# Long convolution with gate: the last 4 of the 100 rows of each a_u store issued by GpSimd instead of SyncE

## The chip, the cores and the metric

The kernel runs on one core of a Trainium2 chip. The core has a matrix engine (TensorE, PE in the profile), a vector engine (VectorE, DVE), an activation engine (ScalarE, ACT), a general engine (GpSimd, POOL) and an engine that only issues transfers and waits (SyncE, SP). Sixteen DMA engines carry the transfers between the chip's large memory (DRAM) and the core's own memory (SBUF). Each compute engine and SyncE works through its own list of instructions in order, and an instruction that has to wait holds up everything behind it on that engine.

The metric is the device time of one execution in microseconds (us); lower is better. The time before is the median of three runs.

## The reference

What is computed, cut to the part that matters:

```python
B, S, D = x.shape                                   # 4, 12800, 128
h_filt = (np.maximum(pos_emb @ w1, 0.0) @ w2) * np.exp(-0.01 * np.arange(S))[:, None]
u = x * v
Uf = np.fft.rfft(u, n=2 * S, axis=1)
Hf = np.fft.rfft(h_filt, n=2 * S, axis=0)
y = np.fft.irfft(Uf * Hf[None], n=2 * S, axis=1)[:, :S]
x = x * y                                           # first half of the work
gate = sigmoid(causal_conv5(x, conv_w))             # second half
out = (gate * (x @ w_val)) @ w_out
```

A long causal convolution along the sequence (12800 positions, 128 channels, 4 batches) is followed by a short gated projection. All arithmetic is in 32-bit floats.

## The kernel before

The long convolution is a Fourier transform that is factored over 100 x 64 positions (`N1 = 100`, `N2 = 64`), and the kernel has three stages, each with its own pools of tiles. The stage boundary goes through DRAM: the first stage writes `a_u`, the second reads `a_u` and writes `c_y`, the third reads `c_y` and writes the result.

**First stage.** It has 64 steps, one for each pair (`q`, `s`) with `q` from 0 to 31 and `s` 0 or 1. A step does the following.

- `fetch(n + 7)` issues a transfer of 1024 KB of `xv` (the inputs x and v) from SyncE into one of five buffers (`held`, shown as the tile `ld`).
- `product(n + 3)` multiplies x and v on DVE (line 312).
- `mirrored(q + 1)`, in every other step, forms sums and differences on DVE (line 321, tile `eo`) and a subtraction for each of the two on POOL (line 322).
- `spectra(q, s)` runs matmuls against a constant table (line 334, into `fp`), and ACT copies the result into the tile `st` (line 336). `st` has four buffers (`bufs=4`): the copy of step n needs the store of step n - 4 landed.
- Some work of the filter's own transform is slipped in (`filt()`), so many units to a step: `gp`, `ap` and `ag` are its tiles, and `fk` its tables.
- `store` writes the 100 rows of `st` of the step before to `a_u[:, s, q]`. A row is 2 x 2 x 4 x 128 floats, or 8 KB.

The 100 rows are not stored in one transfer. The helper `_Split` (lines 109 to 118) cuts them into rows 0 to 95 and rows 96 to 99, two transfers of 768 KB and 32 KB, both on SyncE; the profile therefore shows both at the helper's line 118. The same helper, as `sync_s`, serves the loads of `c_y` in the third stage.

**What sets the order.** The stage is inside `tc.manual_schedule()`: each engine gets its instructions in the order in which the code is written. Waits are put in by the framework. A transfer reports its landing on one of eight counters that are handed out in turn (DMAHW0 to DMAHW7 in the listings of the order; the transfers that GpSimd issues have eight of their own, DMASW0 to DMASW7), and a transfer waits until the one that had its counter before has landed. So at most eight transfers of SyncE are under way at a time in this stage. With three transfers a step (fetch, store of 96 rows, store of 4 rows) that is two steps and two thirds.

**End of the stage.** The first loads of `a_u` for the second stage (`load_pair(0, 24)` and `load_a`, line 213) stand in SyncE's list among the last stores; each waits for the stores of the rows that it reads.

Of the kernel before, what the change touches and what calls it, by code (L numbers as in the profile page):

```python
# [24 lines left out]
J, N1, N2 = 2, 100, 64  # L25
# [96 lines left out]
def tile_longconv_gate(  # L122
# [20 lines left out]
    nc = tc.nc  # L143
    sync_s = _Split(nc.sync)
# [4 lines left out]
    a_u = dram.tile([N1, 2, N2 // 2, 2, J, B, D], F32, name="a_u")  # L149
# [82 lines left out]
    with tc.tile_pool(name="p1", bufs=1) as p1, tc.tile_pool(name="ps1", bufs=1, space=PSUM) as ps1:  # L232
# [92 lines left out]
        def spectra(q, s):  # L325
            eo = eos[q]
            st = p1.tile([128, 2, J, B, D], F32, name="st", bufs=4)
            for o in range(2):
                fp = ps1.tile([128, 2, J, XE], F32, name="fp", bufs=2)
                terms = ((0, 0), (2, 1)) if s == o else ((1, 0),)  # L330
                for i, (w, l) in enumerate(terms):
                    for h in range(2):
                        r = slice(h * NH, (h + 1) * NH)
                        nc.tensor.matmul(  # L334
                            out=fp[:, h], lhsT=fold[r, w], rhs=eo[r, o, :, l], start=i == 0, stop=i == len(terms) - 1)
                nc.scalar.copy(out=st[:, o].rearrange("k j (h b) d -> k h j (b d)", h=2), in_=fp)  # L336
            return st

        def store(q, s, st):
            sync_s.dma_start(  # L340
                out=a_u[:, s, q].rearrange("k e j b d -> k (e j b d)"),
                in_=st[:N1].rearrange("k e j b d -> k (e j b d)"))

        fetched, us, eos, last = {}, {}, {}, None
        with tc.manual_schedule():
# [15 lines left out]
            for n in range(N2):  # L361
                q, s = divmod(n, 2)
                if n + XB + 2 < N2:
                    fetch(n + XB + 2)
                if n + 3 < N2:
                    product(n + 3)
                if s == 0 and q + 1 < N2 // 2:
                    mirrored(q + 1)
                st = spectra(q, s)
                while spent < n_fil * (n + 1) / (N2 - 6):  # L370
                    step = next(fil, None)
                    if step is None:
                        break
                    spent += step
                if n == N2 - 2:
                    loaded[0] = load_pair(0, NL)
                if last:
                    store(*last)
                last = q, s, st
                if n == 40:  # L380
                    _narrow(nc, p1, wval, raw_val)
                if n == 46:
                    _narrow(nc, p1, wout, raw_out)
                if n == 52:
                    _narrow(nc, p1, cw, raw_cw)
            for _ in fil:
                pass
            store(*last)


    with tc.tile_pool(name="p2", bufs=1) as p2, tc.tile_pool(name="ps2", bufs=1, space=PSUM) as ps2:
# [67 lines left out]
        with tc.manual_schedule():  # L459
            for p in range(-1, NP + 1):  # L460
# [8 lines left out]
                if p == 41:  # L469
                    j, g = y_order[0]  # L470
                    nc.sync.dma_start(
                        out=xr_first, in_=xt[j][:, g * R:(g + 1) * R].rearrange("d n b a -> d (n b a)"))
# [57 lines left out]
    with tc.tile_pool(name="p3", bufs=1) as p3, tc.tile_pool(name="ps3", bufs=1, space=PSUM) as ps3:  # L530
# [144 lines left out]
        with tc.manual_schedule():  # L675
# [4 lines left out]
            for _ in range(WARM):  # L680
                w_ps = ps3.tile([D, 2 * D], F32, name="o_ps", bufs=2)
                nc.tensor.matmul(
                    out=w_ps, lhsT=ident, rhs=dft.rearrange("p a k -> p (a k)"), start=True, stop=True)
            for t in range(-AHEAD3, NT + 2):
                s = t + AHEAD3
                if s + 1 < NT:
                    load_rows(s + 1)
                if 0 <= s < NT:
                    j, g = y_order[s]
# [80 lines left out]
```

## Time and profile before

| | |
|---|---|
| time, median of 3 runs | 1163.94 us (1157.94 to 1168.69) |
| the profiled execution, its own time | 1167.67 us |
| its span, first to last instruction | 1165.5 us |
| TensorE clock granted, mean | 0.969 |
| PE, DVE, POOL, ACT busy | 90%, 83%, 67%, 53% of the span |
| bytes moved | 344.60 MB, 296 GB/s over the span |

The span lies within the profiled execution's own time; 2.2 us of that time lie outside the span. A row of the profile that groups instructions gives the line of the kernel, the engine, the operation, the tiles (output, an arrow, inputs), their shapes, a count, then the busy time and the mean duration, and after the bar the idle time of the engine just before them with what ended it. SPq is SyncE issuing transfers. In the table by stretches, each row is a stretch of time with the busy time of each engine, the granted clock, the mean busy share of the 16 DMA engines, and the rate at which they moved bytes; a share can come out above 1 where packets overlap. A packet of a DMA engine is the unit in which the profile counts transfers. In the chain of waits a piece "DMA a_u<-st" runs from the issue of a transfer to its landing.

### The profile page before, as it was taken

The page shows a single profiled execution, that of the slowest core. Times are in us where ns is not written, and L with a number is a line of the kernel's source. Part 1 is how long each engine was busy: PE and PEld are TensorE (multiplying, and loading weights), DVE is VectorE, ACT ScalarE, POOL GpSimd, SP SyncE. Part 2 cuts the span into 40 slices and gives each one's busy share as a digit, 9 for nine tenths or more (in the row PEclk, how much of TensorE's full clock was granted, in tenths as well). Part 3 has the DMA queues.
Part 4 walks back from the last instruction along what each step waited for, and adds up shares of the span by engine and source line. Part 5 has one row for each costly group of instructions (what it writes and reads, how often), then busy time and mean ns, then how long its engine had stood idle before and what let it go on. Part 6 is the DMA issues. An engine that isn't in the chain of part 4 may idle for free.

```text
span 1165.5 us, 17562 instructions
## 1 busy us (share of the span) xinstructions
PE 1046.1 (90%) x6208; PEld 492.1 (42%) x6208; DVE 969.3 (83%) x1150; ACT 615.7 (53%) x1000; POOL 775.2 (67%) x393
## 2 busy tenths in 40 slices
PE   4899887887764999999999999979999999999986
PEld 2455543443321444444444444434444444444432
DVE  5675445798944899999999999629999999999996
ACT  1366555665641344444444444346676767677763
POOL 3354332323313888889888889737889898898880
PEclk9999999998995899999999999988999999999999
DMA  9999999999987588988888998558999999999932
GB/s 364 350 417 403 361 352 345 353 341 350 344 268 286 209 311 300 317 300 302 303 312 287 362 339 321 178 176 218 283 288 285 264 292 278 278 289 284 284 119 113
DMA packets 92888, 344.60 MB, mean 296 GB/s; under 512 B 9774, under 2 KB 19418, under 8 KB 77610
## 3 DMA queue, kind: packets, MB, share of 16 engines
q1 hardware_dynamic: 58824, 263.74, 69.1%
q10 hardware_dynamic: 33978, 79.74, 17.8%
q8 instruction: 51, 0.84, 0.3%
q14 instruction: 35, 0.29, 0.1%
HBM read 212.37 MB, written 131.07 MB: 295 GB/s over the span
## 4 chain that ended last, share of the span: by engine, by line
PE 58%; DMA 28%; ACT 6%; DVE 4%; issue 2%; SPq 1%; ACTq 0%; DVEq 0%
PE c_ps L435 21%; DMA a_u<-st 19%; PE sd L596 9%; PE z_ps L419 9%; DMA ld<-in_xv_dram 6%; PE o_ps L657 6%; PE v_ps L647 5%; PE tp L610 5%; PE c_ps L404 2%; DVE gt L638 2%; PE fp L334 2%; ACT gt L635 1%; ACT o_sb L665 1%; DMA c_y<-c_sb 1%; ACT sg L642 1%
## 5 line engine op out<-in xcount | busy, mean ns | idle before, releaser
L623 POOL TENSOR_TENSOR ext<-yr,xr 128x400 f32<-128x400 f32 x120 | 301.6, 2515 | 44.0 <-DVE yr L621 41.9
L322 POOL TENSOR_TENSOR eo<-eo 128x512 f32<-128x512 f32 x62 | 116.8, 1904 | 212.0 <-DVE eo L321 212.0
L334 PE MATMUL fp<-eo,fold 64*128 64x512 f32 x768 | 194.4, 640 | 54.5 <-ACT st L336 40.1
L638 DVE SCALAR_TENSOR_TENSOR gt<-ext,cw,gt 128x1600 f32<-128x1600 f32 x128 | 241.5, 1887 | 0.8 <-ACT gt L635 0.8
L442 ACT COPY c_sb<-c_ps 128x1024 f32<-128x1024 f32 x100 | 101.3, 1013 | 204.6 <-PE c_ps L435 196.5
L336 ACT COPY st<-fp 128x1024 f32<-128x1024 f32 x128 | 124.2, 1015 | 133.2 <-DMA a_u<-st 81.5
L435 PE MATMUL c_ps<-va,ld 64*128 64x512 f32 (+1 forms) x800 | 166.6, 556 | 0.1
L425 DVE TENSOR_TENSOR va<-z_ps,h_sb 128x2048 f32<-128x2048 f32 x50 | 114.3, 2286 | 38.7 <-DMA ld<-a_u 30.4
L504 POOL TENSOR_TENSOR va<-va,vb 128x1024 f32<-128x1024 f32 x50 | 118.4, 2367 | 40.0 <-DVE vb L425 40.0
L419 PE MATMUL z_ps<-ld 64*64 64x512 f32 x800 | 122.4, 621 | 18.2 <-DMA ld<-a_u 16.3
L334 PEld LDWEIGHTS fp<-eo,fold 64*128 64x128 f32 x768 | 74.8, 197 | 135.8 <-issue 76.4
L596 PE MATMUL sd<-ag,inv 100*64 100x512 f32 x512 | 128.7, 620 | 1.6 <-ACT sd_sb L603 1.0
L657 PE MATMUL o_ps<-gd,wout 128*128 128x400 f32 x256 | 112.4, 521 | 19.7 <-DVE gd L652 10.9
L435 PEld LDWEIGHTS c_ps<-va,ld 64*128 64x128 f32 x800 | 74.2, 189 | 113.7 <-issue 110.2
L506 POOL TENSOR_TENSOR va<-va,vb 128x1024 f32<-128x1024 f32 x50 | 118.3, 2367 | 0.0
L603 ACT COPY sd_sb<-sd 128x512 f32<-128x512 f32 x128 | 76.1, 595 | 76.8 <-PE sd L596 54.1
L425 DVE TENSOR_TENSOR vb<-z_ps,h_sb 128x2048 f32<-128x2048 f32 x50 | 114.0, 2280 | 0.0
L647 PE MATMUL v_ps<-ext,wval 128*128 128x400 f32 x256 | 107.1, 500 | 0.0
L435 PE MATMUL c_ps<-vc,ld 64*128 64x512 f32 x400 | 94.2, 589 | 0.0
L610 PEld LDWEIGHTS tp<-ident,sd_sb 128*128 128x128 f32 x512 | 60.1, 144 | 78.9 <-PE sd L596 47.9
L505 POOL TENSOR_TENSOR vc<-vc,vd 128x768 f32<-128x768 f32 x50 | 91.2, 1824 | 2.2 <-issue 0.3
L610 PE MATMUL tp<-ident,sd_sb 128*128 128x128 f32 x512 | 81.9, 286 | 5.4 <-ACT sd_sb L603 3.8
(84 smaller groups left out, 1452.1 us busy)
## 6 DMA issues: line engine op xcount, KB each, us to landing
ld<-in_xv_dram SPq DMA_DIRECT2D x64, 1024.0 KB
c_y<-c_sb ACTq DMA_DIRECT2D x100, 512.0 KB
ld<-a_u SPq DMA_DIRECT2D x49, 1024.0 KB
a_u<-st SPq DMA_DIRECT2D x64, 768.0 KB
ag<-c_y SPq DMA_DIRECT2D x116, 384.0 KB
out_dram<-o_sb ACTq DMA_DIRECT2D x32, 800.0 KB
xr<-in_xt_dram SPq DMA_DIRECT2D x31, 800.0 KB
ld<-in_tab_w_dram SPq DMA_DIRECT2D x12, 768.0 KB
```

What stands on the lines that cost most here:

```text
L334: nc.tensor.matmul(out=fp[:, h], lhsT=fold[r, w], rhs=eo[r, o, :, l], start=i == 0, stop=i == len(terms) - 1)
L336: nc.scalar.copy(out=st[:, o].rearrange("k j (h b) d -> k h j (b d)", h=2), in_=fp)
L419: nc.tensor.matmul(out=zs[c][half[h]], lhsT=wk[half[c], 0, half[h]], rhs=a2[half[c], h, j], start=True, stop=True)
L425: nc.vector.tensor_tensor(out, z.rearrange("p (b d) -> p b d", d=D).unsqueeze(1).to_broadcast([128, n, B, D]), h_sb.unsqueeze(2).to_broadc ...
L435: nc.tensor.matmul(out=c_ps[:, h, 0:n], lhsT=wk[half[h], 1 + c], rhs=vt[half[h]].rearrange("p b d -> p (b d)"), start=(i == 0), stop=(i == ...
L504: nc.gpsimd.tensor_tensor(va[:, 0:2], va[:, 0:2], vb[:, 0:2], op=ALU.add)
L596: nc.tensor.matmul(out=sd[c * N2:(c + 1) * N2], lhsT=inv[:, c], rhs=ct[c][:, r * B * D:(r + 1) * B * D], start=True, stop=True)
L610: nc.tensor.transpose(out=tp[:, b], in_=t[:, b], identity=ident)
L623: nc.gpsimd.tensor_tensor(e[:, r0 + r], yr, xr, op=ALU.mult)
L638: nc.vector.scalar_tensor_tensor(gt, rows(t, k), cw[:, k:k + 1], gt, op0=ALU.mult, op1=ALU.add)
L647: nc.tensor.matmul(out=v_ps, lhsT=wval, rhs=rows(t)[:, r * ROW:(r + 1) * ROW], start=True, stop=True)
L657: nc.tensor.matmul(out=o_ps, lhsT=wout, rhs=gd, start=True, stop=True)
```

## The change

In `store`, the helper is no longer used. Rows 0 to 95 are issued by SyncE as before; rows 96 to 99 are issued by GpSimd. Bytes, rows and destination are the same. The loads of `c_y`, which use the helper too, are untouched.

```diff
         def store(q, s, st):
-            sync_s.dma_start(
-                out=a_u[:, s, q].rearrange("k e j b d -> k (e j b d)"),
-                in_=st[:N1].rearrange("k e j b d -> k (e j b d)"))
+            for eng, r in ((nc.sync, slice(0, 96)), (nc.gpsimd, slice(96, N1))):
+                eng.dma_start(
+                    out=a_u[r, s, q].rearrange("k e j b d -> k (e j b d)"),
+                    in_=st[r].rearrange("k e j b d -> k (e j b d)"))
```

SyncE's list in the middle of the first stage, before the change: a number behind `st` names the copy of a step, a number behind `ld` a buffer of the fetches, and the brackets name what a transfer waits for (a counter's previous transfer, or an engine).

```order
L118 DMA a_u_60<-st_1026 96x2048 [waits DMAHW2_49,Activation_49]
L118 DMA a_u_60<-st_1026 4x2048 [waits DMAHW3_49]
L306 DMA ld_106<-in_xv_dram 128x2048 [waits DMAHW4_49,DVE_49]
L118 DMA a_u_60<-st_1063 96x2048 [waits DMAHW5_49,Activation_49]
L118 DMA a_u_60<-st_1063 4x2048 [waits DMAHW6_49]
L306 DMA ld_102<-in_xv_dram 128x2048 [waits DMAHW7_49,DVE_49]
```

The same place in SyncE's list after the change:

```order
L341 DMA a_u_60<-st_1026 96x2048 [waits DMAHW1_49,Activation_49]
L306 DMA ld_106<-in_xv_dram 128x2048 [waits DMAHW2_49,DVE_49]
L341 DMA a_u_60<-st_1063 96x2048 [waits DMAHW3_49,Activation_49]
L306 DMA ld_102<-in_xv_dram 128x2048 [waits DMAHW4_49,DVE_49]
L341 DMA a_u_60<-st_1097 96x2048 [waits DMAHW5_49,Activation_49]
```

The transfers of 4 rows are gone from it; a step takes two of the eight counters instead of three, so a counter comes round after four steps.

POOL's list at the same place, after the change (before it, the subtractions of `eo` stand there alone, two for every two steps):

```order
L322 TENSOR_TENSOR eo0_110<-eo0_110 128x2x256 [waits DVE_49] x2
L341 DMA a_u_60<-st_1026 4x2048 [waits DMASW1_49,Activation_49]
L341 DMA a_u_60<-st_1063 4x2048 [waits DMASW2_49,Activation_49]
L322 TENSOR_TENSOR eo1_111<-eo1_111 128x2x256 [waits DVE_49] x2
L341 DMA a_u_60<-st_1097 4x2048 [waits DMASW3_49,Activation_49]
L341 DMA a_u_60<-st_1134 4x2048 [waits DMASW4_49,Activation_49]
```

Two transfers of 4 rows now stand between each two pairs of subtractions; each waits for ACT's copy of its `st` and for the GpSimd transfer of eight steps earlier.

## The prediction

> **What bounds the kernel now.** I read the page's chain of waits first, then the table by stretches, then the waits of the stretch that the change touches, and last the packets there. The chain that ended last, by engine and by line:
>
> ```profile
> PE 58%; DMA 28%; ACT 6%; DVE 4%; issue 2%; SPq 1%; ACTq 0%; DVEq 0%
> PE c_ps L435 21%; DMA a_u<-st 19%; PE sd L596 9%; PE z_ps L419 9%; DMA ld<-in_xv_dram 6%; PE o_ps L657 6%; PE v_ps L647 5%; PE tp L610 5%; PE c_ps L404 2%; DVE gt L638 2%; PE fp L334 2%; ACT gt L635 1%; ACT o_sb L665 1%; DMA c_y<-c_sb 1%; ACT sg L642 1%
> ```
>
> The transfers of the first stage hold 25% of the chain (19% stores of a_u, 6% fetches); the later stages are PE's. So transfers set the first stage, some 360 us of the span, and only there does the change act. The table by stretches shows that it has two regimes:
>
> ```profile
> 60.00:120.00 60.00, 56.59 (x562) 33.56 (x562) 38.15 (x30) 38.97 (x45) 29.82 (x14) 1.00 1.01 409
> 120.00:240.00 120.00, 99.54 (x740) 53.79 (x737) 70.97 (x98) 69.98 (x112) 34.70 (x21) 0.96 0.98 351
> 240.00:320.00 80.00, 64.17 (x292) 32.99 (x290) 71.21 (x112) 51.30 (x100) 27.18 (x16) 0.94 0.98 345
> 120.00:320.00 200.00, 163.71 (x1030) 86.78 (x1026) 142.18 (x209) 121.28 (x211) 61.88 (x37) 0.95 0.98 349
> ```
>
> After the length come PE, PEld, DVE, ACT and POOL busy, the clock, the DMA share and GB/s. Up to 120 us the core moves 409 GB/s, then 349, although the mix of transfers is the same and DMA engines look busy all the time (0.98). PE falls from 94% busy to 82%. What the engines wait for between 120 and 320 us:
>
> ```profile
> POOL eo L322 <- DVE eo L321: 138.1, 19, 13.0
> ACT st L336 <- DMA a_u<-st: 60.2, 27, 4.2
> DVE ld L312 <- DMA ld<-in_xv_dram: 16.1, 5, 3.3
> DVE u L312 <- DMA ld<-in_xv_dram: 11.3, 5, 2.6
> ...
> SPq L118 <- DMA ld<-in_xv_dram: 90.8, 38, 3.5
> SPq L306 <- DMA a_u<-st: 59.8, 37, 2.1
> ```
>
> ACT waits 60.2 us for a store to free st, DVE 27.4 us for fetches, and SP 150.6 us of 200 for one of its eight counters. All of that is late landing. The chain shows how late, and what an uncrowded transfer takes:
>
> ```profile
> 148.71 16.37 DMA a_u<-st
> ...
> 165.58 15.20 DMA a_u<-st
> ...
> 340.59 1.35 SPq L213
> ...
> 343.66 11.24 DMA a_u<-st
> ...
> 355.33 4.25 DMA a_u<-st
> ```
>
> In the crowded stretch a store takes 15 to 16 us from issue to landing; the last one, issued when nothing else was left, takes 4.25 us. L213 at 340.59 is the first load of a_u, at the end of the stage.
>
> **Where the 4 rows lie.** The transfers between 133 and 300 us:
>
> ```profile
> DMA packets 8243, 58.38 MB, mean 350 GB/s; under 512 B 1124, under 2 KB 1124, under 8 KB 1124
> ...
> ld<-in_xv_dram SPq DMA_DIRECT2D x32, 1024.0 KB
> a_u<-st SPq DMA_DIRECT2D x31, 768.0 KB
> a_u<-st SPq DMA_DIRECT2D x31, 32.0 KB
> ```
>
> The 1124 packets under 512 B are the reports of landing: the 63 large transfers, at one from each of 16 engines, make 1008, and the 116 left over 31 small transfers are 3.7 each. Beside the reports no packet is under 8 KB, so a row is one packet. The 4 rows are carried by about four engines, not sixteen. A step then loads an engine with (1024 + 768) / 16 = 112 KB, and the four with 120 KB; spread evenly it would be 1824 / 16 = 114 KB. If they are the same four each time, they set the pace while the others run ahead up to eight transfers and then starve, which is what a fall from 409 to 349 GB/s after a while looks like. No row here shows which four they are.
>
> The Trainium skill ("DMA: Bandwidth & Descriptors", section "Why a DMA increments its semaphore by 16 and not by 1") says that a transfer issued by SyncE takes the lowest-numbered engines, as many as divide its rows, and one issued by GpSimd consecutive engines from a cursor that moves on. By that rule the four would be the same before the change and rotate after it; the count of reports above agrees with the number of engines, and nothing in this trace shows the rotation.
>
> **The change part by part.**
>
> *Removed from SP:* 64 issues and their waits for a counter. One issue costs 0.25 to 0.3 us by this row (60 to 320 us, shortest, median, longest, in ns; the longest hold a wait):
>
> ```profile
> L118 SPq DMA_DIRECT2D a_u<-st x101: 245/303/1950, 60.8 to 319.5; - x101
> ```
>
> That is 64 x 0.25 = 16 us of SP's time, taken at 0: SP waits for landings three quarters of the stretch, and that wait stays if the landings are as late. Two of eight counters a step instead of three lets SP run four steps ahead, not 2.7. I take 0 for that too, since the four buffers of st limit the stores to four steps (the 60.2 us wait of ACT); its bounds are 0 and the gain below.
>
> *Added to POOL:* 64 issues. No row shows a transfer issued by GpSimd. From below it is SP's 0.25 us; from above, POOL's idle time: 138.1 us before eo in 120 to 320 us, at 37 steps (349 GB/s x 200 us / 1.868 MB a step) 3.7 us a step. I take it at SP's end, 0.3 to 1 us, which idle time covers, so 0. If it passed 3.7 us, eo would come late and the matmuls of line 334 would wait. The change also puts a wait into POOL's list: a transfer of 4 rows waits for ACT's copy of its st, with the next eo subtractions queued behind it and the matmuls of line 334 behind those. That copy also gives the two fp buffers back, without which the matmuls that last read this eo tile cannot end, so it is over before eo could start, and the wait adds 0.
>
> *Moved:* the 4 rows, to other engines by my premise. Its worth has two ends. **Low end:** only the unevenness goes, and whatever else slows packets after 120 us stays: 200 us x (1 - 114 / 120) = 10 us. **High end:** the rate returns to the 409 GB/s of the first row. From 120 to 240 us that is 120 x (1 - 351 / 409) = 17.0 us (PE, busy 99.54 of 120, leaves 20.5); from 240 to 320 us it would be 80 x (1 - 345 / 409) = 12.5, but DVE is busy 71.21 of 80 and leaves 8.8. Together 25.8 us. I take the middle, **18 us**: an even load removes the cause of the starving, but PE and DVE are then close to full and will not run without gaps. What is late next is PE in 120 to 240 us and DVE after it.
>
> *Before 120 us:* 0, the rate is full there. *After 320 us:* the store at 343.66 takes 11.24 us and the first loads of a_u wait for it; a smaller backlog could give up to 11.24 - 4.25 = 7 us. I take 0, since those loads share its engines, and keep 7 us for the range. Later stages: 0, no instruction of theirs is changed.
>
> Sum: -18 us on the profiled execution, 1167.67 - 18 = 1149.7. That execution lies 3.7 us above the median of the runs, so against the median 1163.94 - 18 = **1146 us**. Its own range is 10 to 33 us less than 1163.94, or 1131 to 1154.
>
> **The rivals.**
>
> *The same four engines again (no change in the load).* The rows are 4 whether SP or POOL issues them, and one row to an engine may start at the first engine for both. Then 120 KB a step stays the pace, only the counters and SP's time are freed, and both were costed at 0: 1158 to 1168 (0 to -5 us for the freed counters, up to +4 for a later issue). For it speaks that no row shows a transfer of POOL; against it, nothing in the trace. The Trainium skill has a rule on this side ("DMA: Bandwidth & Descriptors", section "Issuing engines are not separate DMA queues"): transfers from any issuing engine share the same 16 DMA engines, so issuing from several saves only the sequencer's time. By it alone the sum would be 0.
>
> *All four rows on one engine.* Rows 96 to 99 lie next to each other, and a split by blocks of rows would give them to one engine. It would carry 112 + 32 = 144 KB a step. At 409 / 16 = 25.6 GB/s that is 5.77 us, against 260 us / 50 fetches = 5.2 us between 60 and 320 us (the row below): +0.57 x 50 = +28 us; if packets stay as slow as now, 5.2 x 144 / 120 = 6.24, or +52 us. So 1192 to 1216.
>
> ```profile
> ld<-in_xv_dram SPq DMA_DIRECT2D x50, 1024.0 KB
> ```
>
> It decides as soon as one engine gets more than the 120 KB of now. Against it: the 3.7 reports above show that a split by single rows is what SP gets.
>
> *GpSimd issues too slowly.* Beyond 3.7 us a transfer, each further us costs about 50 us over the stretch (one a step), so 5 us would give +65. Against it, its nearest row, an arithmetic operation, is half of that (mean 1904 ns):
>
> ```profile
> L322 POOL TENSOR_TENSOR eo<-eo 128x512 f32<-128x512 f32 x62 | 116.8, 1904 | 212.0 <-DVE eo L321 212.0
> ```
>
> **How the numbers follow.** The runs before spread by 5 us to either side, about what three runs can resolve; 1% of 1163.94 is 11.6 us, and I call less than that the same. Chances: even load 0.48, same four 0.39, one engine 0.08, slow issue 0.05. With no row on where POOL's transfers land, the even load is ahead only because it alone uses what the fall to 349 GB/s offers. Faster by over 1% (under 1152.3): 0.42 of the even load and 0.03 of the same four, 0.45. Slower: the last two cases, 0.13. Same: 0.42. The range takes in the even load and the same four, 1131 to 1169, and leaves out 0.13 above and 0.05 below.
>
> **What would show it.** Right: GB/s between 120 and 300 us near 390 to 409 instead of 349, stores landing in under 11 us in the chain, ACT's 60.2 us and DVE's 27.4 us of waits well down, and the first load of a_u some 18 us earlier than 340.59. Same four: GB/s and waits as now. One engine: a rate under 330, landings above 16 us. Slow issue: PE or DVE waiting on POOL's eo. The prediction is wrong if the rate does not rise, or if it rises and PE or DVE turns out to be the pace already.

## The result and the profile after

| | before | after |
|---|---|---|
| median of 14 runs, us | 1164.74 | 1158.64 |
| lowest to highest, us | 1157.94 to 1170.52 | 1149.88 to 1160.27 |
| profiled execution, us (its span) | 1167.67 (1165.5) | 1160.27 (1158.3) |
| first load of a_u issued, us from the start | 340.6 | 333.9 |

The ratio is 0.9938, with a 95% interval of 0.9917 to 0.996: the change saves 6.1 us, about a third of the 18 us that were forecast.

All of it lies in the first stage. The loads of a_u by tile, of the profile before (shortest, median and longest issue in ns, then when the first and the last were issued, in us):

```profile
L213 SPq DMA_DIRECT2D ld<-a_u x4: 316/372/1350, 340.6 to 359.6; - x4
```

And of the profile after, with the two kinds of stores:

```profile
L341 POOL DMA_DIRECT2D a_u<-st x64: 518/521/702, 23.8 to 341.1; - x64
L341 SPq DMA_DIRECT2D a_u<-st x64: 303/327/2023, 32.9 to 350.6; - x64
L213 SPq DMA_DIRECT2D ld<-a_u x4: 315/798/1847, 333.9 to 355.0; - x4
```

From the first load to the end it is 1167.67 - 340.6 = 827.1 us before and 1160.27 - 333.9 = 826.4 after. That start is therefore a good measure of the first stage alone, and it is used so below.

The table by stretches of the profile after, with the columns of the one before (length, PE, PEld, DVE, ACT and POOL busy, clock, DMA share, GB/s):

```profile
60.00:120.00 60.00, 55.03 (x524) 31.75 (x526) 35.96 (x28) 35.85 (x42) 27.92 (x24) 0.97 1.01 404
120.00:240.00 120.00, 100.51 (x780) 54.98 (x778) 76.39 (x103) 72.72 (x115) 47.75 (x44) 0.97 0.97 359
120.00:320.00 200.00, 163.59 (x1082) 86.89 (x1082) 146.48 (x217) 126.03 (x216) 83.47 (x76) 0.97 0.97 359
```

The fall after 120 us is still there: 404 GB/s, then 359, where it was 409 and 349. At the same bytes 200 x (1 - 349 / 359) = 5.6 us are saved in that stretch, which is nearly all of the result.

The waits between 120 and 320 us, of the engines and of SP, after the change (total us, times, longest):

```profile
POOL eo L322 <- DVE eo L321: 98.4, 20, 8.0
ACT st L336 <- DMA a_u<-st: 64.4, 34, 3.1
DVE ld L312 <- DMA ld<-in_xv_dram: 17.4, 6, 5.1
POOL a_u L341 <- ACT st L336: 13.7, 5, 3.1
...
DVE u L312 <- DMA ld<-in_xv_dram: 6.8, 5, 1.9
...
SPq L306 <- DVE eo L321: 38.8, 12, 4.5
SPq L306 <- DVE u L312: 27.1, 10, 6.1
SPq L341 <- ACT st L336: 26.0, 12, 4.0
...
SPq L341 <- DMA a_u<-st: 18.3, 12, 1.8
...
SPq L306 <- DMA ld<-in_xv_dram: 14.2, 17, 1.8
```

Two things stand in it. SP's waits for a counter (the rows with DMA) fell from 150.6 to 18.3 + 14.2 = 32.5 us; SP now waits mostly for buffers that DVE and ACT give back. But what the other engines wait for hardly moved: ACT 64.4 us for a store to free st (60.2 before), DVE 17.4 + 6.8 us for fetches (27.4 before).

The transfers between 133 and 300 us after the change:

```profile
DMA packets 9269, 60.23 MB, mean 361 GB/s; under 512 B 1926, under 2 KB 1926, under 8 KB 1926
...
q0 software_dynamic: 1020, 1.03, 2.3%
...
ld<-in_xv_dram SPq DMA_DIRECT2D x32, 1024.0 KB
a_u<-st SPq DMA_DIRECT2D x32, 768.0 KB
a_u<-st POOLq DMA_DIRECT2D x32, 32.0 KB, 6.9
```

64 large transfers with 16 reports each make 1024 of the 1926 small packets; the 902 left over 32 GpSimd transfers are some 28 each. Queue q0 is GpSimd's. Over the whole execution the page gives it 2048 packets and 2.10 MB, which is 32 packets for each of the 64 transfers: four rows of 8 KB and 28 small packets. So four rows still go to at most four engines, now with 28 small packets beside them in place of about four. The Trainium skill ("DMA: Bandwidth & Descriptors", section "Why a DMA increments its semaphore by 16 and not by 1") says that for GpSimd's transfers all 16 engines post a completion, and that on trn2 some direct copies are given all 16 engines with the rows shared out from the first one on. The count has room for these 16 completions; what the other 12 small packets are, no row shows. Which engines get the rows is in no view here either, so whether they change from one transfer to the next had to be found out by runs.

### The profile page after: what moved, and what is told of

Same layout as the page of the kernel before. It is cut to its first block, busy times and chain, and to the rows that moved or that the text cites. A ratio compares the mean times of both kernels' runs of the same rounds, so it can differ in the third digit from the quotient of the medians.

```text
span 1158.3 us, 17638 instructions
## 1 busy us (share of the span) xinstructions
PE 1041.1 (90%) x6208; PEld 486.7 (42%) x6208; DVE 966.5 (83%) x1150; ACT 615.2 (53%) x1000; POOL 801.7 (69%) x457
## 3 DMA queue, kind: packets, MB, share of 16 engines
q0 software_dynamic: 2048, 2.10, 0.7%
## 4 chain that ended last, share of the span: by engine, by line
PE 57%; DMA 27%; ACT 7%; DVE 5%; issue 2%; POOL 0%; SPq 0%; ACTq 0%; DVEq 0%
PE c_ps L436 20%; DMA a_u<-st 19%; PE sd L597 9%; PE z_ps L420 9%; PE o_ps L658 6%; PE v_ps L648 5%; PE tp L611 4%; PE c_ps L405 2%; DMA c_y<-c_sb 2%; DVE gt L639 2%; DMA ld<-in_pos_dram 2%; ACT st L336 2%; PE fp L334 2%; DMA ag<-c_y 1%; ACT o_sb L666 1%
## 5 line engine op out<-in xcount | busy, mean ns | idle before, releaser
L624 POOL TENSOR_TENSOR ext<-yr,xr 128x400 f32<-128x400 f32 x120 | 303.0, 2526 | 40.5 <-DVE yr L622 38.3
L322 POOL TENSOR_TENSOR eo<-eo 128x512 f32<-128x512 f32 x62 | 109.7, 1784 | 157.8 <-DVE eo L321 157.8
```

Source lines behind the costliest of these rows:

```text
L624: nc.gpsimd.tensor_tensor(e[:, r0 + r], yr, xr, op=ALU.mult)
```

## The experiments

Three questions: is an uneven load what paces the stage (F: the few engines with 120 KB a step against 112 KB on the others), what gave the 6 us (C: the freed counters), and does GpSimd use the same engines each time (S) or others in turn (R). Eight kernels were run. The first four are compared with 11 runs of the kernel before (median 1163.36 us), the other four with 17 (1164.57 us); the kernel after was run beside another 14 (1164.74 us), so a difference of 1 to 2 us between the sets says nothing.

| kernel | load of the engines a step | counters a step | us | ratio (95%) | first load of a_u |
|---|---|---|---|---|---|
| before | 112 KB, four with 120 | 3 | 1164.74 | 1 | 340.6 |
| after | 112 KB, at most four with 120 | 2 | 1158.64 | 0.9938 (0.9917 to 0.996) | 333.9 |
| e1_pad112 | 120 KB on all | 2 | 1138.79 | 0.9791 (0.9764 to 0.9819) | 310.0 |
| e2_no_tail | 112 KB on all | 2 | 1128.95 | 0.9702 (0.9675 to 0.973) | 300.7 |
| e3_after_mark | as after | 3 | 1175.56 | 1.0118 (1.0085 to 1.015) | 346.4 |
| e4_four_single | 114 KB on all | 2 | 1138.29 | 0.9788 (0.9757 to 0.9818) | 308.9 |
| e5_after_dup | as after, the 4 rows twice | 2 | 1214.7 | 1.043 (1.0402 to 1.0457) | 380.0 |
| e6_before_dup | as before, the 4 rows twice | 3 | 1199.28 | 1.0293 (1.0266 to 1.032) | 374.9 |
| e7_no_tail_mark | 112 KB on all | 3 | 1129.54 | 0.9704 (0.9679 to 0.9728) | 303.0 |
| e8_short_fetch | meant as 113 KB on all | 2 of SP | 1161.55 | 0.9965 (0.9933 to 0.9997) | 342.7 |

The load of an engine is worked out from the sizes of the transfers, and for e4 and after from their packets; the counters are those of SP.

**e1_pad112: more bytes, but evenly.** a_u gets 112 rows, seven for each of 16 engines, and one transfer stores them:

```diff
-    a_u = dram.tile([N1, 2, N2 // 2, 2, J, B, D], F32, name="a_u")
+    a_u = dram.tile([112, 2, N2 // 2, 2, J, B, D], F32, name="a_u")
...
-            sync_s.dma_start(
+            nc.sync.dma_start(
                 out=a_u[:, s, q].rearrange("k e j b d -> k (e j b d)"),
-                in_=st[:N1].rearrange("k e j b d -> k (e j b d)"))
+                in_=st[:112].rearrange("k e j b d -> k (e j b d)"))
```

> One store of 112 rows a step from SyncE (12 rows of padding that nobody reads), no transfer of 4 rows: every engine carries 64 + 56 = 120 KB a step, and a step takes two counters. Theory F (the 4 rows still go to the same four engines after the change, and their 120 KB set the pace while the others starve): the loaded engines carry as much as now, but none starves; at 409 GB/s a step of 1920 KB takes 4.81 us instead of 5.0 to 5.2, so 1138 to 1155 us. Theory P (the change made the load even and PE and DVE are the pace now): 96 KB more a step bring nothing, 1158 us or more.

Measured 1138.79 us: 24.6 less than before and 20 less than after. The table by stretches of e1:

```profile
60.00:120.00 60.00, 58.35 (x588) 33.84 (x586) 40.10 (x30) 40.82 (x47) 31.18 (x14) 1.00 1.01 423
120.00:240.00 120.00, 105.19 (x764) 57.27 (x762) 88.70 (x121) 80.46 (x135) 43.40 (x24) 0.99 1.01 424
240.00:320.00 80.00, 66.58 (x332) 32.16 (x328) 66.09 (x100) 52.65 (x88) 25.08 (x14) 0.96 1.00 377
```

With 96 KB more a step the fall at 120 us is gone: 424 GB/s where after has 359 (the last row holds the end of the stage, which e1 reaches at 310 us). A step of 1.966 MB then takes 4.64 us, against 1.868 / 359 = 5.20 us. A DMA share of 0.97 and one of 1.01 look alike although the rates are 15% apart. SP's transfers between 133 and 300 us, before and then in e1:

```profile
q1 hardware_dynamic: 8230, 58.22, 97.9%
q1 hardware_dynamic: 9613, 69.50, 100.6%
```

At nearly the same share e1 moves 19% more, that is 16% more for the same packet time. So the rate before isn't lost in engines that stand without a packet, as the prediction's word "starve" has it, but for the most part in packets that take longer. What an engine does in such a packet, whether it waits or moves bytes more slowly, no view shows. ACT's wait for a store is halved:

```profile
ACT st L336 <- DMA a_u<-st: 30.1, 20, 2.8
```

It also shows that one sign named ahead was a bad one. The chain of e1 (start, length in us):

```profile
123.17 16.68 DMA a_u<-st
141.90 17.36 DMA a_u<-st
161.32 16.89 DMA a_u<-st
```

The stores land as late as before, 17 us after issue, in a kernel that is 25 us faster: with four buffers of st queued they probably wait behind each other at any rate. Landing time doesn't tell the uneven load from the even one here.

**e2_no_tail: the four rows away.** Rows 96 to 99 aren't stored, and the last two pairs of the next stage read rows 94 and 95 in their place, so only the time counts:

```diff
-                in_=a_u[2 * p:2 * p + 2].rearrange("k s n e j b d -> (s n e) k (j b d)"))
+                in_=a_u[2 * min(p, 47):2 * min(p, 47) + 2].rearrange("k s n e j b d -> (s n e) k (j b d)"))
...
-            sync_s.dma_start(
-                out=a_u[:, s, q].rearrange("k e j b d -> k (e j b d)"),
-                in_=st[:N1].rearrange("k e j b d -> k (e j b d)"))
+            nc.sync.dma_start(
+                out=a_u[0:96, s, q].rearrange("k e j b d -> k (e j b d)"),
+                in_=st[:96].rearrange("k e j b d -> k (e j b d)"))
```

> Rows 96 to 99 of a_u are not stored at all, and the last two pairs of the second stage read rows 94 and 95 instead; 112 KB on every engine, two counters a step. F: the uneven load is gone, 1792 KB a step at 409 GB/s are 4.49 us, held back by PE and DVE: 1130 to 1148 us. P: the load was even already, 1155 to 1159 us.

Measured 1128.95 us, 34.4 less than before for 32 KB less a step (1.8%). Its busiest stretch:

```profile
120.00:240.00 120.00, 110.89 (x799) 60.26 (x800) 99.16 (x132) 87.60 (x144) 44.16 (x26) 1.00 1.01 415
```

PE is busy 92% and DVE 83% there, beside DMA engines that are still full (1.01): PE and DVE come close to being the bound. Between e1 and e2, both even, 8 KB an engine and step cost 10 us; between e2 and after, 8 KB on a few engines cost 30.

**e3_after_mark: the third counter back.** Behind each store SP also writes four values of 4 bytes to a scratch tile, so that a step takes three of SP's counters again, at next to no bytes:

```diff
+    mark = dram.tile([N2, 4, 1], F32, name="mark")
...
+            nc.sync.dma_start(out=mark[2 * q + s], in_=ident[0:4, 0:1])
```

> The changed kernel, with one more transfer on SyncE behind each store: 4 rows of 4 bytes to a scratch tensor. A step takes three counters and three issues of SyncE again; the 4 rows of a_u stay with GpSimd. Theory C (the 6 us come from the freed counters): back to 1162 to 1167 us. F without C, or P: 1157 to 1160 us, as the changed kernel.

Measured 1175.56 us: 17 us more than after, and 12 more than before. SP's waits are what they were before the change:

```profile
SPq L345 <- DMA ld<-in_xv_dram: 78.2, 37, 3.3
SPq L307 <- DMA a_u<-st: 65.5, 37, 2.5
```

and the rate falls earlier than in either kernel:

```profile
60.00:120.00 60.00, 51.91 (x478) 29.68 (x476) 37.20 (x28) 34.02 (x40) 31.09 (x24) 0.97 0.99 364
120.00:320.00 200.00, 163.52 (x1096) 87.04 (x1092) 142.21 (x208) 123.12 (x210) 80.59 (x73) 0.96 0.98 352
```

So with the third transfer and its counter the gain is gone, which is the way C points; but C had 1162 to 1167 us, and the time goes 9 us beyond that. From 120 us on the rate is that of before (352 against 349), and the loss lies in the 364 GB/s ahead of it. Whether that comes of the four rows on GpSimd's queue or of the mark's own small packets was not separated, so the 17 us are not the price of a counter alone.

**e7_no_tail_mark: the third counter under an even load.** The edits of e2 and e3 together; rows 96 to 99 are left out as in e2.

> No transfer of 4 rows (rows 96 to 99 are not stored, the last two pairs read rows 94 and 95), and behind each store of SyncE a transfer of 4 rows of 4 bytes, so a step takes three counters: even load of 112 KB. With two counters the same load took 1129 us. If a third counter costs what it cost the changed kernel (17 us), 1146 us; if it costs only where some engines run late (fewer transfers in flight leave the others without work), 1129 to 1136 us.

Measured 1129.54 us against 1128.95 of e2: the mark and its counter cost nothing here, and 17 us in e3. So a third transfer a step costs time only together with the uneven load. A likely reason is that the counter of a transfer comes back when its slowest engine is done, so with fewer transfers of work in flight the other engines can't run as far ahead of a late one; the reports below fit that.

**e4_four_single: the four rows as four transfers of one row on GpSimd.**

```diff
-            for eng, r in ((nc.sync, slice(0, 96)), (nc.gpsimd, slice(96, N1))):
+            for eng, r in ((nc.sync, slice(0, 96)), *((nc.gpsimd, slice(k, k + 1)) for k in range(96, N1))):
```

> The 4 rows as four GpSimd transfers of one row each. If each starts at the same engine (F), that one carries 112 + 32 = 144 KB a step: 1185 us or more. If a cursor moves on, the load is even at 114 KB: 1150 us or less if an uneven load is the pace, about 1158 us if PE and DVE are (P). GpSimd's issue, 0.52 us in the changed kernel's trace, is paid four times a step and fits its idle time in all cases.

Measured 1138.29 us, 25 less than before and 20 less than after, with the same bytes. The packets of e4 between 133 and 300 us:

```profile
DMA packets 13299, 65.81 MB, mean 394 GB/s; under 512 B 3272, under 2 KB 5407, under 8 KB 5407
...
a_u<-st SPq DMA_DIRECT2D x34, 768.0 KB
a_u<-st POOLq DMA_DIRECT2D x136, 8.0 KB, 6.4
```

5407 - 3272 = 2135 packets of 512 B or more over 136 transfers are 15.7 each: a row of 8 KB goes out in 16 pieces of 512 B, by the count one for an engine. So the load is even because each row is split, and nothing is learned here of a rotation. But it is the change under study with an even load: the same rows by the same queue, and the rate holds. Since e4 is 20 us faster than the kernel after, the load after was not even.

```profile
120.00:240.00 120.00, 106.54 (x770) 57.82 (x766) 90.25 (x122) 82.00 (x136) 91.15 (x123) 0.99 1.01 407
```

**e5_after_dup and e6_before_dup: the four rows twice.** GpSimd copies rows 96 to 99 once more to a scratch tile, in e5 behind its own transfer of the kernel after, in e6 beside SP's store of the kernel before:

```diff
+            nc.gpsimd.dma_start(
+                out=more[:, s, q].rearrange("k e j b d -> k (e j b d)"),
+                in_=st[96:N1].rearrange("k e j b d -> k (e j b d)"))
```

> The changed kernel with the GpSimd transfer of 4 rows issued a second time, to a scratch tensor (32 KB more a step; SyncE's list is as in the changed kernel). Theory S (each GpSimd transfer of 4 rows goes to the same four engines): they carry 128 KB a step instead of 120, 6.7% more over the 200 to 260 us that they pace, 1171 to 1176 us. Theory R (its four engines change from one to the next): 2 KB more on every engine, 1160 to 1164 us.

> The kernel before (both parts of the store on SyncE) with the 4 rows also sent by GpSimd to a scratch tensor. If GpSimd's four engines are the four that SyncE uses: 128 KB on them, 1176 to 1181 us. If they are four others, or change: the heaviest load stays near 120 KB, 1163 to 1168 us.

Measured 1214.7 us for e5, 56 more than after, and 1199.28 for e6, 35 more than before, for 32 KB a step (1.8% of its bytes). The stretch of e5, then of e6:

```profile
120.00:320.00 200.00, 155.19 (x1104) 83.36 (x1102) 117.88 (x166) 109.72 (x177) 93.10 (x104) 0.93 0.93 330
```

```profile
120.00:320.00 200.00, 154.57 (x1080) 82.62 (x1076) 117.28 (x170) 109.36 (x180) 74.55 (x69) 0.94 0.96 329
```

A step of 1.900 MB takes 5.76 us at 330 GB/s and 5.78 at 329. If the second copy goes to the engines that carry the first, these have 128 KB a step: 128 / 120 x 5.20 = 5.55 us for e5 and 128 / 120 x 1.868 / 349 = 5.71 us for e6. On other engines it would by this sum have cost next to nothing, 120 KB staying the most that any has; and the number of GpSimd's transfers alone costs nothing, as the four a store of e4 show. R, which had 1160 to 1164 us for e5, doesn't hold. But both times also lie above what a shared set of engines had (1171 to 1176 us for e5, 1176 to 1181 for e6), by 39 and 18 us: the direction fits S, and the size is explained by neither. A second copy that loads all engines alike was not run.

**e8_short_fetch: no gain.** On top of e1 the fetch reads only 114 of 128 rows, 112 by SP and two by GpSimd as single rows; the other 14 are zeros, set once:

```diff
-            nc.sync.dma_start(out=t, in_=xv[n_seq[i]].rearrange("h q w j l b d -> (h q) (w j l b d)"))
+            src = xv[n_seq[i]].rearrange("h q w j l b d -> (h q) (w j l b d)")
+            for eng, r in ((nc.sync, slice(0, 112)), (nc.gpsimd, slice(112, 113)), (nc.gpsimd, slice(113, 114))):
+                eng.dma_start(out=t[r], in_=src[r])
...
+            for i, t in enumerate(held):
+                (nc.vector if i % 2 == 0 else nc.gpsimd).memset(t[96:128], 0.0)
```

> The padded store of 112 rows, and fetches without their last 14 rows, which are zeros: 112 rows by SyncE, 2 rows by GpSimd as single rows; the zeros are set once. 56 + 56 + 1 = 113 KB on every engine instead of 120. F: between the padded store (1139 us) and no transfer of 4 rows (1129 us), 1128 to 1134 us. Over 1139 us if GpSimd's two more transfers a step hold up its subtractions.

Measured 1161.55 us, 23 more than e1 with 112 KB less a step. Its stretch:

```profile
120.00:320.00 200.00, 170.11 (x1207) 92.38 (x1206) 145.47 (x208) 129.72 (x216) 105.88 (x117) 0.98 1.01 376
```

The DMA engines are busy all the time (1.01) at only 376 GB/s, so here too packets take longer. The reason that was allowed for, late subtractions of GpSimd, is not it: between 120 and 320 us the matmuls wait for them 1.3 us in all.

```profile
PEld fp L336 <- POOL eo L324: 1.3, 5, 0.5
```

Fetches now also stand in GpSimd's list behind its other work, and they are loads in pieces of 512 B; which of the two it is stays open.

**When each engine reports.** The packed traces keep the moment of each report of landing, though no view of the profile prints it: 16 for a large transfer of SP, one from each engine. Where more than 3 us lie between one report of a transfer and the next, the next and those behind it are called late here. The large transfers whose first report came between 133 and 300 us:

| kernel | engines on time, then late | first to last report, us: median (range) |
|---|---|---|
| before | 13, then 3 | 9.0 (7.6 to 9.9) |
| after | half of the transfers 12, then 2 and 2; most others 14, then 2 | 13.1 (8.4 to 16.0) |
| e1_pad112 | 16 | 4.4 (3.1 to 5.7) |
| e2_no_tail | 16 (2 of 72: 15, then 1) | 5.2 (2.5 to 7.9) |
| e3_after_mark | 15, then 1 | 8.3 (6.9 to 9.8) |
| e4_four_single | 16 | 4.5 (3.0 to 6.3) |
| e5_after_dup | 12 to 14, then the others one or two at a time | 16.1 (13.4 to 19.9) |
| e6_before_dup | 14, then 2 | 9.9 (8.5 to 12.9) |
| e7_no_tail_mark | 16 (25 of 70: 15, then 1) | 6.1 (2.1 to 8.5) |
| e8_short_fetch | 16 (23 of 58: 15, then 1) | 8.6 (0.8 to 11.8) |

With the four rows uneven, one to four engines are late in nearly every large transfer; with the even loads of e1 and e4 none is. In the kernel before, the first late reports come at 108 us and from 133 us on every transfer has them, which is about where the rate falls; in the kernel after, they begin at 84 us. Rows that went to other engines each time would have given every engine the same over a few steps, and a group of two to four engines would hardly have stayed this far behind for 200 us. So S holds: GpSimd's four rows load a few fixed engines, and a second copy of them makes these later still (16.1 us against 13.1). In e6 two engines are late and never more, which fits a set shared with SP's rows; which engines they are, the traces don't say. e7 and e8 have single late engines too, and why is not known; e8's load, meant to be even, is in any case not even in time.

Not tried: more buffers of st with the change.

## Why the prediction was wrong

**The step that failed** is the part headed "Moved": "the 4 rows, to other engines by my premise", and the even load of 0.48 that rested on it. The rows did change the queue, but the load stayed uneven. A GpSimd transfer of four rows still has four packets of data; after the change two to four engines still report late, now 13.1 us from first to last report where it was 9.0; and the same rows cut into pieces for all engines (e4) are 20 us faster. "The same four engines again" is the rival that describes what happened: its 1158 to 1168 us hold the measured 1158.64, and its sign, "GB/s and waits as now", is nearly what the tables show. That the measured time also lies in the stated range, 1131 to 1169, says little, since the range took in both cases; the sum of 18 us was for the wrong one.

**The rules weighed there.** The moving cursor of the Trainium skill ("DMA: Bandwidth & Descriptors", section "Why a DMA increments its semaphore by 16 and not by 1") is not what this copy of four rows does, by the late engines of the table above; the same section's exception for direct copies, with all 16 engines and the rows from the first one on, fits better. The Trainium skill's other rule (the same page, section "Issuing engines are not separate DMA queues") came nearer: by it alone the sum would have been 0, and the change brought 6 us. It speaks of the sequencer's time only, and these 6 us are more likely from the counters (below).

**The diagnosis of the bound** held, and its mechanism in part. An uneven load holds up the first stage, and an even one is worth what the high end of the sum gave, 25.8 us: e4 measured 25 us with the very same bytes, e1 24.6 with more; against the kernel after, which has two counters a step as they have, it is 20. The middle of 18 us was too low for that case because the low end took only bytes into account. The bytes don't explain it: in e1 every engine carries 120 KB in 4.64 us, while after needs 5.20 us with 120 KB on a few. Nor do the others starve in the sense of having no packet (the share is 0.97 to 0.98): packets take longer, and what else is lost beside a late engine was not settled. PE and DVE did not become the pace either; in e1 the DMA engines are full at 424 GB/s, above the 409 that the high end took for the full rate.

**Counters, taken at 0 "since the four buffers of st limit the stores to four steps".** This is probably the term that came out otherwise, 6 us where 0 was put and the rival allowed 5. SP's waits for counters fell by 118 us, and the others now run further ahead of the late engines, 13.1 us from first to last report where it was 9.0 (8.3 in e3, which has the third counter again). ACT's wait for st stayed, which is that limit, so the gain likely ends there. The chain of the profile after shows it, a copy into st and a store in turn, 19 to 20 us for the four buffers:

```profile
127.71 17.86 DMA a_u<-st
145.67 1.94 ACT st L336 x2
147.62 17.23 DMA a_u<-st
164.95 1.94 ACT st L336 x2
166.90 17.70 DMA a_u<-st
```

That the counters gave the 6 us rests on these waits and on e3, which takes the gain back but adds more than that; it is the reading that fits and not one that a run isolates.

**POOL's issues, 0.3 to 1 us and hidden:** 0.52 us each. Their waits for ACT's copy come to 13.7 us, and POOL still idles 98.4 us before eo. In e4 four issues a store, 0.49 us each, cost nothing that shows. **All four rows on one engine, and a slow issue:** neither happened. **After 320 us, 0:** right, the last full store takes 12.26 us and the time from the first load of a_u on is the same to 0.7 us:

```profile
337.89 12.26 DMA a_u<-st
350.23 0.32 SPq L213
350.64 4.34 DMA a_u<-st
```

**Before 120 us, 0 "the rate is full there":** nearly right for this change (404 against 409 GB/s), though an even load has 420 to 423 there (e1, e2, e4).

## What to carry to other kernels

Where a stage is bound by transfers, try giving each store a number of rows that 16 divides, by padding if need be: 12 more rows made this kernel 25 us faster, and moving the odd 4 rows to another queue made it 6 us faster. Before costing a transfer on another queue, count its row packets, which bound the number of engines that carry them, and look at the reports of the large transfers beside it: a few engines that stay late for many steps are loaded each time. A busy share near 1 doesn't say that the rate is full, so compare it with the rate when the bytes are spread evenly; and don't read the landing time of a queued store as a sign of an uneven load.

## What the runs showed of the hardware that was not expected

- A small uneven part costs far beyond its bytes: 32 KB more a step on a few engines cost 35 to 56 us (e6, e5), while 96 KB more, spread so that all carry 120 KB, came with 25 us less than before (e1).
- With 4 rows of 100 uneven, a few engines report 6 us and more behind the others for some 200 us, first to last 9.0 us before and 13.1 after; with the load even it is 4.4 (e1) and 4.5 (e4).
- A third transfer a step of next to no bytes, with its counter, cost 17 us with an uneven load (e3 against after) and nothing with an even one (e7 against e2).
- A GpSimd transfer of 4 rows has 28 small packets beside its rows, SP's about 4; the one lands after 6.9 us (median) while SP's stores take 17 us in the chain.
- A busy share of 1.01 went with 424 GB/s in e1 and with 376 in e8, where part of the fetch came in pieces of 512 B.
